# A local-attention and two-MoE kernel on one core: load pieces, a scheduler that counts TensorE's instruction blocks, new keys, and an unused tile

## The chip, the core and the metric

The kernel runs on one core of a Trainium2 chip. A time is device microseconds (us) of one execution. Beside it stands one execution under the hardware profiler, whose trace gives every number on single instructions. TensorE is PE, its weight loads PEld, VectorE DVE, ScalarE ACT, GpSimd POOL, and SyncE SP; all loads that matter here are issued from SP's queue. A PE matmul in the trace comes with one weight load: the text calls the two a pair, which is two instructions.

## The reference

Three layers in float32, with 4 batches, 8 heads of 64, 512 local and 32 global positions.

```python
# layer 1: local queries see +-32 positions and the 32 global keys; global queries see all
s_g = scale * q_g @ k_all.T;  out_g = softmax(s_g) @ v_all
s_ll = where(abs(i - j) <= 32, scale * q_l @ k_l.T, -1e9);  s_lg = scale * q_l @ k_g.T
out_l = softmax(concat([s_lg, s_ll])) @ concat([v_g, v_l])
x = concat([out_g, out_l]) as [4, 576, 512]
# layer 2, d_ff 1024
h = maximum(x @ w_in, 0)
gate = sigmoid(conv3(h, conv_w))         # three taps along the sequence
x = (h * gate) @ w_out
# layer 3
xk, xr = mu_k * x + (1 - mu_k) * x_prev, mu_r * x + (1 - mu_r) * x_prev
out = sigmoid(xr @ w_r) * (maximum(xk @ w_k, 0) ** 2 @ w_v)
```

## The kernel before

**Work.** A unit u is one batch and two heads; there are 16, four to a batch. `attend(u)` makes the scores `s` (32 small matmuls in float32, 64 pairs in the trace), masks them (DVE), takes exponents (ACT), transposes them (`pe`, 4 pairs for each of two heads), multiplies by the values (`o`, 32 pairs a head), normalises into `xn` (DVE) and transposes that into `X` (4 pairs). `glob(u)` does the global queries of units u-1 and u, on odd u: `sg` (8 pairs), the exponents `eg` with their normalisation, `peg` (3 pairs, twice) and `Xg` (48 pairs). Layer 2 multiplies by w_in into `ph` and by w_out into `po`; layer 3 is `pk`, `pr` and `pv` in chunks of 384 tokens. Each float32 weight is split into two parts (`_hi`, `_lo`), and so are the activations, with three matmuls for each product.

**Weights.** A piece of 512 columns of a weight is one DMA (`fload`, 511.8 KB). POOL clears a buffer for its magnitude (`fzero`), ACT takes the absolute value (L733), DVE puts the low words to it (L737), and then the two parts are rounded out (L786, L789).

**Order.** Every step is a `Task` with an engine, a cost in ns, keys, and the buffers that it takes; `Plan.schedule` puts all tasks into one order at build time by a model of the engines' times. `s_key` gives each unit its due time from T_START, STEP0, SLOT and GAP; LAG_TE, LAG_PV, LAG_G and LAG_TX give the later steps of a unit theirs. A task that needs another ACT table is put back by PENALTY. Some steps have a second engine in `alts`, and DVE_BIAS, ACT_BIAS and POOL_BIAS weigh that choice by phase of the kernel. `Clock` models TensorE's clock; where it would fall, or where a wait is long, `warm` puts fillers in front of a task: matmuls on the identity whose result is thrown away (L381). The DMAs are in this order too, so the plan sets which load stands ahead of which in SP's queue. q and k have three buffers each, as v has.

**Data.** The host lays out q, k and v so that one unit's q is 2,304 bytes for each of 128 partitions, k 2,688 and v 7,280, each in one piece.

## Time and profile before

| | us |
|---|---|
| median of 3 runs | 556.32 |
| lowest, highest | 555.46, 558.76 |
| the profiled execution's own time | 557.58 |
| its span, first to last instruction | 555.8 |
| PE busy in the span | 531.0 (96%) |

The profiled execution is 1.26 us above the median, and 1.78 us of it lie outside the span. Times of the trace count from the span's start.

### The profile page before, as it was taken

How to read it: one execution, taken by the hardware profiler on the slowest of the kernel's cores; microseconds unless marked ns; L12 is line 12 of the kernel's file. 1: busy time of each engine (PE TensorE's matmuls, PEld its weight loads, DVE VectorE, ACT ScalarE, POOL GpSimd, SP SyncE). 2: the span in 40 equal slices, each digit the busy share in tenths (PEclk: the TensorE clock that was granted, in tenths of full speed). 3: DMA queues.
4: the chain of work that ended last, by engine and by line, in shares of the span. 5: the costliest groups of instructions: out<-in, count | busy, mean ns of one | idle time of the engine just before them, and what ended most of it. 6: DMA issues, size and time to landing. Idle time of an engine off the chain costs nothing.

```text
span 555.8 us, 13782 instructions
## 1 busy us (share of the span) xinstructions
PE 531.0 (96%) x5502; PEld 487.0 (88%) x5502; DVE 348.0 (63%) x956; ACT 250.9 (45%) x562; POOL 150.7 (27%) x308
## 2 busy tenths in 40 slices
PE   7688979999999799999999999999999999999997
PEld 6576977999999799999999988898898898898896
DVE  4586969635994449952599699499245457245131
ACT  5588979855877458862796673001001001001000
POOL 4323355211021100110100110000077477276060
PEclk9797989999999899999999999999999999999999
DMA  8887706668328501101516641201201200100101
GB/s 313 348 281 285 275 7 218 225 214 285 129 88 285 192 31 50 68 22 43 172 59 196 205 130 44 85 1 44 72 1 28 77 0 20 57 2 0 58 2 38
DMA packets 30593, 64.61 MB, mean 116 GB/s; under 512 B 4672, under 2 KB 16704, under 8 KB 30528
## 3 DMA queue, kind: packets, MB, share of 16 engines
q1 hardware_dynamic: 28224, 59.26, 31.8%
q10 hardware_dynamic: 2304, 4.47, 2.1%
q8 instruction: 43, 0.70, 0.5%
q14 instruction: 22, 0.18, 0.1%
HBM read 51.64 MB, written 12.07 MB: 115 GB/s over the span
## 4 chain that ended last, share of the span: by engine, by line
PE 73%; DVE 9%; DMA 8%; ACT 3%; issue 3%; POOL 2%; SPq 1%; ACTq 0%; DVEq 0%; POOLq 0%
PE pv L1189 17%; PE pk L1086 16%; PE po L949 11%; PE ph L848 9%; PE pr L1152 9%; DMA kT<-in_k_l_dram 3%; DVE c L890 3%; PE s L488 2%; PE o L529 2%; PE pe L519 2%; PE Xg L671 2%; PE sg L612 1%; DMA wkk<-wkkd 1%; DMA v<-in_v_l_dram 1%; PE X L560 1%
## 5 line engine op out<-in xcount | busy, mean ns | idle before, releaser
L848 PE MATMUL ph<-x,win_hi 128*128 128x256 f32 (+1 forms) x512 | 99.3, 292 | 0.0
L848 PEld LDWEIGHTS ph<-x,win_hi 128*128 128x128 f32 x512 | 79.9, 188 | 1.0 <-issue 0.6
L949 PE MATMUL po<-gh,wout_hi 128*128 128x288 f32 (+1 forms) x256 | 77.3, 302 | 0.2 <-issue 0.2
L949 PE MATMUL po<-gl,wout_hi 128*128 128x288 f32 (+1 forms) x256 | 75.0, 293 | 0.6 <-DVE gl L911 0.6
L949 PE MATMUL po<-gh,wout_lo 128*128 128x288 f32 (+1 forms) x256 | 74.5, 291 | 0.0
L848 PE MATMUL ph<-x,win_lo 128*128 128x288 f32 (+1 forms) x256 | 73.4, 287 | 0.0
L1086 PE MATMUL pk<-xkh,wkk_hi 128*128 128x384 f32 (+1 forms) x192 | 62.8, 327 | 0.9 <-ACT xkh L1045 0.9
L1086 PE MATMUL pk<-xkl,wkk_hi 128*128 128x384 f32 (+1 forms) x192 | 62.8, 327 | 0.2 <-DVE xkl L1049 0.2
L1086 PE MATMUL pk<-xkh,wkk_lo 128*128 128x384 f32 (+1 forms) x192 | 62.8, 327 | 0.0
L1167 ACT ACTIVATE robuf<-pr 128x512 f32<-128x512 f32 x17 | 10.2, 599 | 114.8 <-PE pr L1152 112.6
L890 DVE SCALAR_TENSOR_TENSOR c<-h,convw,c 128x544 f32<-128x544 f32 x64 | 50.4, 805 | 6.8 <-ACT c L883 6.3
L1189 PE MATMUL pv<-wvv_lo,k2h 128*128 128x512 f32 (+1 forms) x144 | 54.4, 378 | 0.0
L1189 PE MATMUL pv<-wvv_hi,k2h 128*128 128x512 f32 (+1 forms) x144 | 54.4, 378 | 0.0
L1189 PE MATMUL pv<-wvv_hi,k2l 128*128 128x512 f32 (+1 forms) x144 | 54.4, 377 | 0.0
L1109 POOL TENSOR_TENSOR robuf<-robuf 128x384 f32<-128x384 f32 (+1 forms) x32 | 25.2, 791 | 100.2 <-DVE robuf L1106 100.0
L949 PEld LDWEIGHTS po<-gh,wout_hi 128*128 128x128 f32 x256 | 49.3, 193 | 1.3 <-issue 0.8
L949 PEld LDWEIGHTS po<-gl,wout_hi 128*128 128x128 f32 x256 | 49.3, 193 | 0.9 <-DVE gl L911 0.8
L949 PEld LDWEIGHTS po<-gh,wout_lo 128*128 128x128 f32 x256 | 49.2, 192 | 0.0
L848 PEld LDWEIGHTS ph<-x,win_lo 128*128 128x128 f32 x256 | 48.2, 188 | 0.0
L1202 DVE TENSOR_TENSOR robuf<-pv,robuf 128x512 f32<-128x512 f32 (+1 forms) x18 | 11.9, 662 | 55.4 <-PE pv L1189 38.0
L510 ACT ACTIVATE e<-e 128x128 f32<-128x128 f32 x128 | 40.1, 394 | 10.2 <-DVE e L503 7.8
L1152 PE MATMUL pr<-wrr_hi,xrbuf 128*128 128x512 f32 x136 | 43.7, 395 | 0.0
(188 smaller groups left out, 1127.7 us busy)
## 6 DMA issues: line engine op xcount, KB each, us to landing
v<-in_v_l_dram SPq DMA_DIRECT2D x16, 910.0 KB, 6.9
kT<-in_k_l_dram SPq DMA_DIRECT2D x16, 336.0 KB, 6.1
qT<-in_q_l_dram SPq DMA_DIRECT2D x16, 288.0 KB, 5.3
x2d<-xo ACTq DMA_DIRECT2D x16, 272.5 KB, 3.5
out_dram<-robuf SPq DMA_DIRECT2D x16, 256.0 KB, 2.0
wout_0r<-in_moe_w_out_dram SPq DMA_DIRECT2D x8, 511.8 KB, 4.3
wkk<-wkkd SPq DMA_DIRECT2D x8, 256.0 KB, 3.2
win_0r<-in_moe_w_in_dram SPq DMA_DIRECT2D x4, 511.8 KB, 9.1
```

Source lines behind the costliest of these rows:

```text
L488: nc.tensor.matmul(s[a][32 * j : 32 * j + 32, i], lhsT=qT[rows[a], q : q + 32], rhs=kT[rows[a], c : c + P], start=(i == 0), stop=True, ski ...
L510: nc.scalar.activation(be.tile[:, P * i : P * (i + 1)], be.tile[:, P * i : P * (i + 1)], AF.Exp, bias=be.tile[:, SL + i : SL + i + 1], sca ...
L519: nc.tensor.transpose(pt[:, i], be.tile[:, P * i : P * (i + 1)], ident)
L529: nc.tensor.matmul(o[32 * j : 32 * j + 32, i], lhsT=bt.tile[:, i, 32 * j : 32 * j + 32], rhs=v[:, a, first_block(4 * i + j)], start=(i == ...
L848: nc.tensor.matmul(pm, lhsT=w[:, k, P * m : P * (m + 1)], rhs=x[:, s0:s1], start=(k == 0 and n == 0), stop=(k == KT - 1 and n == 2),)
L890: e.scalar_tensor_tensor(bc.tile, bh.tile[:, k : k + S], convw[:, FT * k + m : FT * k + m + 1], bc.tile, op0=ALU.mult, op1=ALU.add,)
L949: nc.tensor.matmul(pm, lhsT=w[:, k, P * m : P * (m + 1)], rhs=g[:, k % 2, s0:s1], start=(k == 0 and n == 0), stop=(k == FT - 1 and n == 2),)
L1086: nc.tensor.matmul(bp.tile[:, :n], lhsT=w[:, k, P * m : P * (m + 1)], rhs=x[:, :n], start=(k == 0 and i == 0), stop=(k == KT - 1 and i == 2),)
L1109: e.tensor_mul(ks()[:, :n], kk()[:, :n], kk()[:, :n])
L1152: nc.tensor.matmul(bp.tile, lhsT=x[:, P * j : P * (j + 1)], rhs=w[:, k], start=(k == 0 and i == 0), stop=(k == KT - 1 and i == 2),)
L1189: nc.tensor.matmul(bp.tile, lhsT=x, rhs=w[:, k, c0:c1], start=(k == 0 and i == 0), stop=(k == FT - 1 and i == 2),)
L1202: nc.vector.tensor_mul(o()[:, c0:c1], bp.tile, r()[:, c0:c1])
```

## The change

1. **Pieces.** A helper `runs` loads k in two pieces for each partition (1,344 bytes each) and v in four (1,820 bytes each); the host lays k and v out accordingly. q stays in one piece. Each is still one DMA. A 512-column weight load becomes two DMAs, of 2,048 and 2,046 bytes for each partition.
2. **The scheduler.** A class `Fetch` counts the instructions of PE tasks (ROWS) in blocks of 256; where a block is entered, it notes when the one after it would be ready (FETCH, or FETCH_BUSY with loads under way), and a task that crosses into a block that isn't ready gets the difference added to its end.
3. **Numbers.** New keys, lags, biases, filler constants, and costs of `s`, `gs`, `pv`, `gpv`, `zero` and `abs`; LAG_TE goes from 3,470 to -2,216, LAG_PV from 12,390 to 18,256, PENALTY from 587 to 1,360, FILL_MIN from 0 to 336.
4. **A tile.** A tile `edge` of 8 float32 columns stands first in the pool of the second MoE's weights. Nothing writes or reads it. In the built program it has no address, and `wrr_hi` stands at byte 206,816 of a partition and `wrr_lo` at 215,008 in both kernels, which is 32 above a multiple of 64.

```diff
-T_START = 9268
-STEP0 = 4976
+T_START = 9166
+STEP0 = 5715
...
-LAG_TE = 3470
-LAG_PV = 12390
+LAG_TE = -2216
+LAG_PV = 18256
-S_COST = 1330
+S_COST = 880
-FILL_MIN = 0
-FILL_MARGIN = 212
+FILL_MIN = 336
+FILL_MARGIN = 92
-PENALTY = 587
+PENALTY = 1360
+FETCH = 1500
+FETCH_BUSY = 2800
...
                 t.end = clock.run(e, t.cost, t.weight, True)
+                t.end += fetch.run(t.kind, e, t.end, free["DMA"], True)
...
+ROWS = {"s": 128, "pv": 64, "te": 8, "tx": 8, "gt": 6, "gs": 16, "gpv": 192, "warm": 6}
+BLOCK = 256
+class Fetch:
+    def __init__(self):
+        self.rows, self.asked, self.ready = 104.0, 0, {}
+    def run(self, kind, start, end, dma, commit):
+        n = ROWS.get(kind, 12)
+        rows, stall = self.rows, 0.0
+        ready = self.ready if commit else dict(self.ready)
+        for k in range(int(rows // BLOCK) + 1, int((rows + n) // BLOCK) + 1):
+            x = start + (k * BLOCK - rows) / n * (end - start) + stall
+            stall += max(0.0, ready.get(k, 0.0) - x)
+            x = max(x, ready.get(k, 0.0))
+            ready[k + 1] = x + (FETCH_BUSY if dma > x else FETCH)
+        if commit:
+            self.rows = rows + n
+        return stall
...
+    def runs(tile, src):
+        n = src.shape[0]
+        nc.sync.dma_start(out=tile.rearrange("p (c e) -> p c e", c=n), in_=src.rearrange("c p e -> p c e"))
...
-            nc.sync.dma_start(out=halves[:, : 4 * n - 1], in_=skewed(src))
+            part, words = skewed(src), 4 * n - 1
+            step = 4 * EST
+            for c in range(0, words, step):
+                end = min(c + step, words)
+                nc.sync.dma_start(out=halves[:, c:end], in_=part[:, c:end])
...
+                w2["p"].tile([P, 8], F32, tag="edge", name="edge")
...
-        "q_l": q, "k_l": k, "v_l": v,
+        "q_l": runs(q, 1), "k_l": runs(k, 2), "v_l": runs(v.reshape(NU, P, -1), 4),
```

Three places show how the order moves. In them `s3_0` is the scores of unit 3, first head; `pe1_1` the transposes of unit 1, second head; `kT3` and `qT3` are its k and q. A number behind the last underscore is the built program's own and differs between the kernels.

On SP, at the start of the program, behind q0, k0, q1 and k1. Before:

```order
L470 DMA v0_193<-in_v_l_dram 128x1820
L470 DMA v1_231<-in_v_l_dram 128x1820
L464 DMA qT2_282<-in_q_l_dram 128x576
L464 DMA kT2_284<-in_k_l_dram 128x672
L724 DMA win0_0r_297<-in_moe_w_in_dram 128x2047
L724 DMA win1_0r_324<-in_moe_w_in_dram 128x2047
L464 DMA qT3_337<-in_q_l_dram 128x576
L464 DMA kT3_346<-in_k_l_dram 128x672
```

Now:

```order
L491 DMA v0_193<-in_v_l_dram 128x4x455
L491 DMA qT2_271<-in_q_l_dram 128x576
L491 DMA kT2_278<-in_k_l_dram 128x2x336
L491 DMA v1_284<-in_v_l_dram 128x4x455
L762 DMA win0_0r_347<-in_moe_w_in_dram 128x1024
L762 DMA win0_0r_347<-in_moe_w_in_dram 128x1023
L762 DMA win1_0r_354<-in_moe_w_in_dram 128x1024
L762 DMA win1_0r_354<-in_moe_w_in_dram 128x1023
L491 DMA qT3_379<-in_q_l_dram 128x576
L491 DMA kT3_395<-in_k_l_dram 128x2x336
```

q2 and k2 now stand ahead of v1, and the two weight pieces are four DMAs; the bytes ahead of k3 are the same.

On PE, in the first units, behind the first head's `o` of unit 1 (`o1_0`). Before, where the scores of unit 2 follow `o1_0`, then those of unit 3 from here on:

```order
L488 MATMUL s3_0_464<-kT3_346,qT3_337 32x128 x4
L488 MATMUL s3_1_465<-kT3_346,qT3_337 32x128 x4
...
L519 MATMUL pe1_1_515<-ident_94,e1_1_303 128x128 x4
L656 MATMUL peg1_0_521<-ident_94,eg1_309 128x128 x3
L560 MATMUL X0_527<-ident_94,xn0_395 128x128 x4
L519 MATMUL pe2_0_541<-ident_94,e2_0_498 128x128 x4
```

Now, where unit 2's scores stand ahead, right behind `sg1`:

```order
L563 MATMUL o1_0_447<-v1_284,eT1_0_424 32x65 x16
L553 MATMUL pe1_1_473<-ident_94,e1_1_298 128x128 x4
L553 MATMUL pe2_0_482<-ident_94,e2_0_372 128x128 x4
L553 MATMUL pe2_1_493<-ident_94,e2_1_390 128x128 x4
L690 MATMUL peg1_0_499<-ident_94,eg1_341 128x128 x3
L522 MATMUL s3_0_503<-kT3_395,qT3_379 32x128 x4
L522 MATMUL s3_1_504<-kT3_395,qT3_379 32x128 x4
```

Four groups of transposes that stood behind the scores of unit 3 stand ahead of them.

On PE, among the matmuls of the second batch of layer 2. Before, where these four steps follow each other with no dense matmul between them (each row of `s` stands for the eight of its unit):

```order
L671 MATMUL Xg11_3234<-egT11_3202,v11_2700 64x32 x12
L529 MATMUL o11_0_3264<-v11_2700,eT11_0_3170 32x65 x16
L529 MATMUL o11_1_3289<-v11_2700,eT11_1_3187 32x65 x16
L488 MATMUL s12_0_3310<-kT12_2460,qT12_2442 32x128 x4
...
L488 MATMUL s13_0_3349<-kT13_3088,qT13_3070 32x128 x4
...
L949 MATMUL po1_2_1_3217<-gh1_4_2828,wout_hi_170 128x288
```

Now s12 and s13 stand apart, each between dense matmuls, and s10 and s11 stand together:

```order
L705 MATMUL Xg9_2595<-egT9_2547,v9_2319 64x32 x12
L563 MATMUL o9_0_2623<-v9_2319,eT9_0_2478 32x65 x16
L563 MATMUL o9_1_2645<-v9_2319,eT9_1_2495 32x65 x16
L886 MATMUL ph1_4_1_2581<-x0_6_1326,win_hi_160 128x288
...
L886 MATMUL ph1_5_0_2680<-x0_5_174,win_lo_161 128x256
L522 MATMUL s10_0_2695<-kT10_1929,qT10_1918 32x128 x4
...
L522 MATMUL s11_0_2733<-kT11_2445,qT11_2430 32x128 x4
...
L886 MATMUL ph1_5_0_2680<-x0_6_1326,win_hi_160 128x256
```

The run of 240 pairs with only attention work is cut up; in its place stands one of 112 and, 12 dense matmuls later, one of 128.

## Rows read from the trace of the kernel before

**Rows 1.** The page's first part: each engine's busy us, share, instructions.

```profile
PE 531.0 (96%) x5502; PEld 487.0 (88%) x5502; DVE 348.0 (63%) x956; ACT 250.9 (45%) x562; POOL 150.7 (27%) x308
```

**Rows 2.** PE's waits over the whole span: line, releaser, total us, times, longest.

```profile
PE s L488 <- DMA kT<-in_k_l_dram: 4.9, 4, 3.0
PE s L488 <- issue: 4.6, 2, 3.4
PE X L560 <- DVE xn L541: 2.1, 2, 1.5
PE peg L656 <- DVE xn L540: 1.8, 1, 1.8
...
PE Xg L671 <- issue: 0.9, 1, 0.9
```

**Rows 3.** Busy time by stretch: length, engines, granted clock, DMA share, GB/s.

```profile
0.00:104.00 104.00, 87.54 (x1652) 76.32 (x1652) 77.29 (x280) 81.33 (x185) 42.33 (x95) 0.92 0.67 244
104.00:320.00 216.00, 211.99 (x2676) 204.41 (x2665) 143.20 (x402) 143.73 (x323) 22.88 (x111) 0.99 0.43 139
```

**Rows 4.** The same view, four stretches at half clock: the last, the sum.

```profile
188.99:192.40 3.41, 3.41 (x16) 3.41 (x16) 1.84 (x17) 0.57 (x2) 0.50 (x9) 0.50 0.23 79
sum 20.47, PE 18.23 PEld 15.46 DVE 12.62 ACT 12.35 POOL 9.67; mean PE 4.56 PEld 3.86 DVE 3.16 ACT 3.09 POOL 2.42
```

**Rows 5.** The timeline of PE from 14 to 21 us, idle before in brackets.

```profile
14.40 1.15 PE L488 MATMUL s<-kT,qT 64*32 64x128 f32 x64 [0.23 <-DMA kT<-in_k_l_dram]
18.50 1.07 PE L488 MATMUL s<-kT,qT 64*32 64x128 f32 x23 [2.96 <-DMA kT<-in_k_l_dram]
20.74 0.68 PE L488 MATMUL s<-kT,qT 64*32 64x128 f32 x16 [1.16 <-issue]
```

**Rows 6.** The same view from 36 to 48 us.

```profile
39.16 0.55 PE L656 MATMUL peg<-ident,eg 128*128 128x128 f32 x3 [1.75 <-DVE xn L540]
39.54 0.39 PE L381 MATMUL s<-ident 128*128 128x128 f32 x2
```

**Rows 7.** DMA from 0 to 40 us: GB/s in 40 slices, then issues.

```profile
GB/s 0 65 277 323 325 289 405 410 400 422 403 397 374 301 395 400 451 437 382 407 400 418 401 373 362 291 83 0 62 327 278 386 256 291 397 355 255 244 191 304
...
v<-in_v_l_dram SPq DMA_DIRECT2D x5, 910.0 KB, 8.4
kT<-in_k_l_dram SPq DMA_DIRECT2D x7, 336.0 KB, 8.1
```

**Rows 8.** ACT's groups from 0 to 104 us, one of its table loads.

```profile
L510 ACT ACT_TABLE_LOAD x3 | 3.8, 1283 | 0.8 <-PEq L1322 0.7
```

**Rows 9.** Busy time by stretch, 80 to 100 us.

```profile
80.00:100.00 20.00, 19.17 (x338) 17.08 (x338) 18.82 (x55) 19.20 (x39) 9.33 (x13) 0.92 0.58 199
```

**Rows 10.** The timeline of PE from 181 to 190 us.

```profile
183.03 1.74 PE L488 MATMUL s<-kT,qT 64*32 64x128 f32 x104
188.17 0.64 PE L488 MATMUL s<-kT,qT 64*32 64x128 f32 x24 [3.39 <-issue]
```

**Rows 11.** The instruction queue: on the page, then at 185.85 to 186.9 us.

```profile
q8 instruction: 43, 0.70, 0.5%
...
q8 instruction: 1, 0.02, 5.6%
```

**Rows 12.** Busy time and counts from the start and from pause to pause.

```profile
0.00:20.74 20.74, 12.64 (x349) 10.21 (x349) 11.20 (x68) 11.29 (x30) 7.17 (x30) 0.94 0.91 345
20.74:46.92 26.18, 22.07 (x507) 18.65 (x506) 19.02 (x85) 20.06 (x51) 7.69 (x15) 0.89 0.76 264
46.92:96.36 49.44, 45.71 (x634) 40.88 (x634) 40.52 (x110) 43.84 (x90) 24.84 (x44) 0.91 0.53 197
96.36:188.17 91.81, 87.89 (x1392) 83.56 (x1393) 59.33 (x202) 64.62 (x157) 14.60 (x58) 1.00 0.64 209
```

**Rows 13.** PE's groups by form, from 342 us on.

```profile
L1189 PE MATMUL pv<-wvv_lo,k2h 128*128 128x512 f32 x128 | 49.9, 389 | 0.0
...
L1152 PE MATMUL pr<-wrr_hi,xrbuf 128*128 128x512 f32 x113 | 36.4, 395 | 0.0
```

## The prediction

> **What bounds the kernel now.** I read the page's busy times first: PE is busy 531.0 of 555.8 us [rows 1], so the time is PE's matmuls plus what PE loses, and no other engine's sum matters by itself. Then busy time by stretch: in the first 104 us PE is busy 87.54, in the next 216 it is busy 211.99 [rows 3]. The losses sit at the start, where four units of attention wait for loads and for DVE and ACT, and in a few places later. The waits of PE name them: 4.9 us for k loads, 2.1 and 1.8 for `xn` from DVE, and 4.6 us of `s` and 0.9 of `Xg` in which PE waited for nothing that the profile shows [rows 2]. These last ones are of another kind: in the timeline two of them, 1.16 and 3.39 us, stand in the middle of one unit's scores, whose operands are all there [rows 5, 10].

> What they have in common is a count. From the start to the first such pause there are 349 pairs, from there 507, 634 and 1,392 [rows 12] (the third ends in a pause of 0.23 us). Doubled, the last three are 1,014, 1,268 and 2,784 instructions: just under 4, 5 and 11 times 256, and the rest is PE's instructions that leave no matmul record. The instruction queue moved 43 packets, 0.70 MB [rows 11], and 11,004 instructions of PE [rows 1] over 43 is 256. One such packet lies inside the 3.39 us pause [rows 11]. So I take these pauses as PE out of instructions: a block of 256 isn't there when the one before is used up. A block with attention work alone is 128 pairs, and scores go at 104 pairs in 1.74 us [rows 10], so it lasts 2.1 us; 128 pairs before the pause PE was at about 182.6 (24 pairs, some 0.4 us, ahead of 183.03), and it went on at 188.17. The next block thus came some 5.5 us after the one before it was entered, with two v loads behind each other in the queues. [...]

> [...]

> **The change part by part.** The sum is made against the profiled execution, 557.58, which is 1.26 above the median of 556.32; I take the difference off both.

> *The start.* (a) `s3` waits 2.96 us for its k [rows 5]. Before, the transposes pe1_1, peg1_0, pe2_0 and pe2_1 come behind it; now they stand ahead, since the scores of unit 2 are earlier and k2 is loaded ahead of v1. Four groups at peg's 0.55 us [rows 6] are 2.2 us moved into a wait. Against it stands that k3 may land later. The bytes ahead of it are the same, but in shorter pieces: with q and k loads alone (slices 3 to 6) 277 to 325 GB/s move, with v loads behind them (slices 7 to 12) about 405 [rows 7]. If short pieces go at 304, a v load of 910 KB takes 3.0 instead of 2.25 us, 0.75 more, and two stand ahead of k3: 0 to +1.5. The slow slices also hold the queue's start, so I take the middle, 0.8. Net -1.4. (b) peg3_0 waits 1.75 us, by the row for `xn` on DVE [rows 6]; ahead of `xn` DVE also normalises `eg3`, which peg3_0 needs. In the changed kernel ACT does that step, right behind the copy of X1. I take half: -0.9. (c) From 80 to 100 us ACT is busy 19.20 of 20 [rows 9], so work taken from ACT there is time. A table load is 1.28 us [rows 8]. Up to there the new order has 7 of them instead of 9; later it has 12 more, where ACT waits for PE and they cost nothing (that cover gone, they would cost up to 15). 2 x 1.28 = 2.6, of which half on the path: -1.3. Together -3.6. The bounds are wide, as half of this region is reordered: at best another 5 us of its 16.5 without PE work, -8.6; at worst two new waits as long as that for `xn`, +3.

> *The pause at 184.78.* s12 and s13 now stand apart, each between dense matmuls, so no block there is short: -3.39 - 1.7 = **-5.1**. What is late next is nothing that this trace shows: behind it the stretch to 320 us loses little else.

> *New short blocks.* Counting blocks of 256 along the new order, I find three with almost only attention work: six `ph`, s10 and most of s11 (2.7 us); Xg7, half of o8 and s9 (2.8 us); s14, s15 and Xg13 (2.85 us). The first is the worst, as in it two v buffers have just been given back by Xg9 and o9, so v loads run. If a block still takes 5.5 us there, the pause is 2.8 and the clock costs 1.7 again: +4.5. If it takes under 2.7, nothing. The nearest row is the pause with two v loads [rows 10], but those moved 7,280 bytes at a time and these 1,820. I take a third: **+1.5** for the three together, from 0 to 4.5 for one. [...]

> *Other loads and issue.* PE's other k waits are 1.9 us in total [rows 2]; the loads of w_in feed ACT and DVE. Later by up to a quarter of a k load's 8.1 us [rows 7]: 0 to +2.0, and I take **+0.5**. SP issues two DMAs for a weight piece instead of one; its queue waits for buffers most of the time, which covers this, and where it doesn't, the next load starts later by one issue, within the bound just named.

> *Fillers.* The new plan has 11 instead of 3. Two take 0.39 us [rows 6], so eight more are 1.6 us; most stand in waits. **+0.4**, from 0 to 1.6.

> *The tile* is never written or read, and the weights' addresses are the same: **0**. The plan's count is off as well: it counts 192 for each `Xg`, where the trace has 48 pairs, 96. So its idea of where a block begins is wrong behind every `Xg`, and only partly does it do what it is for. Layer 3's order is unchanged, and PE waits for nothing there: 0.

> Sum: -3.6 - 5.1 + 1.5 + 0.5 + 0.4 = -6.3, so 551.3 for the profiled execution and **550.0** against the median.

> **The rivals.** *The start absorbs its gain* (553.6): between 80 and 100 us DVE is busy 18.82 and ACT 19.20 of 20 [rows 9], so what PE gains before is waited for again there, and -3.6 falls away. Speaking for it is how tight that stretch is; against it, that ACT has fewer table loads.

> *Slower, by the blocks* (562.0): if a block still takes 5.5 us, all three short blocks pause: 3 x (2.8 + 1.7) = 13.5 instead of 1.5, so 550.0 + 12.0. At 3.7 us a block it would be no change: 3 x (0.9 + 1.7) is what is gained elsewhere. For it speaks that the plan's count is wrong; against it the shorter pieces, and that two of the three blocks have few loads about them.

> *The pauses aren't fetches* (553.6): PE waited for something else that the v loads cause, the pause comes back wherever these now fall, and the -5.1 and the +1.5 both go. For it speaks that the longest pause stands right behind two v loads; the count of 256 and the packet inside the pause speak against it. [...]

> *The tile works after all* (548.7), that is, the other direction of "does nothing": `pr` takes 395 ns a matmul and `pv`, whose weights stand on a multiple of 64, 389 [rows 13]. If it moved the tiles, 204 matmuls by 6 ns are 1.3 us less.

> **How the numbers follow.** Chances: forecast 0.54, start absorbed 0.24, slower by blocks 0.12, not fetches 0.06, tile 0.04. The forecast's own range is 545 to 554, and the likeliest value 550.0. The range for 8 in 10 is 544.5 to 558.5: it takes in the absorbed start and the worst single block, and leaves out the slower rival and the best of the start. Within 1% (about what a measurement can tell from no change) is 550.8 to 561.9. Of the forecast's 0.54 some 0.38 lies below 550.8, as its start has more room to gain than to lose; with the tile, faster is 0.42. Slower is its rival's 0.12, and the rest, 0.46, is within 1%.

> **What would show it.** After: the wait of `s` for "issue" without a pause over 1 us around 184; `s3`'s wait for k under 1.5 us; ACT's busy time from 80 to 100 us below 19; layer 3 as before, `pr` at 395. Wrong would be: pauses in the middle of s11, s9 or Xg13, each behind an instruction packet that lands late; k3 landing over 2 us later; or a new wait between 60 and 104 us as long as what the start gained.

## The result, and the profile after

The changed kernel takes 548.7 us (median of 4 runs, 547.92 to 550.56) against 556.72 for the kernel before: a ratio of 0.9895, with an interval of 0.9852 to 0.9938. By the ratio that is 5.9 us less; 6.3 were forecast. The ratio is not the quotient of the two medians, which is 0.9856 (8.0 us) and lies inside the interval. Nine more runs gave 0.9904 (0.9868 to 0.9940). Executions over 1.5% above the fastest of their kernel are left out of all ratios; two of them, one of b_short and one of i_nofill, took 856 us at a mean clock of 0.557. The profiled execution took 550.56, its span is 548.8.

The first part of the page and PE's waits (line, releaser, total us, times, longest) in the changed kernel, to be held against [rows 1, 2]:

```profile
PE 530.2 (97%) x5518; PEld 486.8 (89%) x5518; DVE 323.0 (59%) x896; ACT 288.9 (53%) x631; POOL 144.8 (26%) x309
```

```profile
PE s L522 <- DMA kT<-in_k_l_dram: 4.4, 3, 2.2
PE X L594 <- issue: 2.5, 1, 2.5
PE s L522 <- issue: 2.2, 3, 1.2
PE pk L1124 <- ACT xkh L1083: 1.4, 1, 1.4
PE pe L410 <- DVE egT L695: 1.4, 1, 1.4
...
PE X L594 <- DVE xn L575: 0.2, 1, 0.2
```

The 3.39 us pause is gone. The waits that name `xn` went from 2.1 and 1.8 to 0.2 (1.7 in the trace of after_again), the one for `eg` from 1.4 to 0.3. But the waits for k are almost what they were, 4.4 instead of 4.9, and PE still waits 4.7 us for "issue" in two groups, against 5.5 before.

Where PE's idle time went is best seen in two stretches. Busy time by stretch, before and then changed:

```profile
0.00:36.00 36.00, 27.90 (x642) 23.33 (x646) 21.49 (x121) 22.69 (x61) 10.71 (x38) 0.91 0.86 321
36.00:104.00 68.00, 59.64 (x1022) 52.99 (x1014) 55.80 (x160) 58.64 (x125) 31.62 (x57) 0.92 0.58 204
```

```profile
0.00:36.00 36.00, 27.21 (x640) 22.45 (x640) 19.39 (x105) 21.35 (x58) 11.44 (x39) 0.86 0.86 300
36.00:104.00 68.00, 65.12 (x985) 59.24 (x977) 58.23 (x185) 61.91 (x138) 22.49 (x52) 0.97 0.65 218
```

In the first 36 us nothing is gained: 640 matmuls instead of 642. From 36 to 104 us PE is idle 2.9 instead of 8.4 us (4.4 in the trace of after_again). The timeline of PE in the changed kernel shows why the first stretch stood still (idle before in brackets):

```profile
9.58 1.14 PE L646 MATMUL sg<-kT,qT 128*64 128x480 f32 x8
12.53 0.70 PE L522 MATMUL s<-kT,qT 64*32 64x128 f32 x33 [1.82 <-DMA kT<-in_k_l_dram]
...
20.29 0.41 PE L522 MATMUL s<-kT,qT 64*32 64x128 f32 x5
21.41 1.21 PE L522 MATMUL s<-kT,qT 64*32 64x128 f32 x59 [0.71 <-issue]
22.54 1.12 PE L563 MATMUL o<-v,eT 128*32 128x65 f32 x64
23.59 0.55 PE L690 MATMUL peg<-ident,eg 128*128 128x128 f32 x3
26.62 0.60 PE L594 MATMUL X<-ident,xn 128*128 128x128 f32 x4 [2.48 <-issue]
...
44.67 0.83 PE L410 MATMUL pe<-ident 128*128 128x128 f32 x6
...
143.37 1.96 PE L522 MATMUL s<-kT,qT 64*32 64x128 f32 x120
146.50 0.42 PE L522 MATMUL s<-kT,qT 64*32 64x128 f32 x8 [1.16 <-issue]
```

`s3` (20.29) no longer waits for its k, as it did for 2.96 us [rows 5]. Instead `s2`, which now stands ahead, waits 1.82 for k2 behind `sg1`, and a new pause of 2.48 us stands in front of the first transposes into X, those of X0 (the expectations below call the place X1). Between the two "issue" pauses lie 59 + 64 + 3 = 126 pairs, a block of 128 within what the rows resolve at its edges. The new short block of the forecast is there too, after 120 of the 128 pairs of s10 and s11. The row at 44.67 is three fillers; the text comes back to it.

### The profile page after: what moved, and what is told of

It reads as the page before. It is cut to its first block, busy times and chain, and to the rows that moved or that the text cites. A ratio compares the mean times of both kernels' runs of the same rounds, so it can differ in the third digit from the quotient of the medians.

```text
span 548.8 us, 13843 instructions
## 1 busy us (share of the span) xinstructions
PE 530.2 (97%) x5518; PEld 486.8 (89%) x5518; DVE 323.0 (59%) x896; ACT 288.9 (53%) x631; POOL 144.8 (26%) x309
## 4 chain that ended last, share of the span: by engine, by line
PE 42%; DVE 4%; ACT 2%; DMA 1%; issue 1%; ACTq 0%; DVEq 0%
PE pv L1227 17%; PE pk L1124 16%; PE pr L1190 9%; DMA wvv_0r<-in_moe_w_v_dram 1%; DVE c L928 1%; ACT c L921 1%; DMA wvv_256r<-in_moe_w_v_dram 1%; DVE gl L949 0%; ACT h L910 0%; DVE xkl L1087 0%; DVE wrr_lo L827 0%; DVE xt0xr L1073 0%; ACT c L934 0%; DVE xrbuf L1101 0%; DVE d L1061 0%
## 5 line engine op out<-in xcount | busy, mean ns | idle before, releaser
L886 PE MATMUL ph<-x,win_hi 128*128 128x288 f32 (+1 forms) x512 | 99.1, 292 | 0.0
L987 PE MATMUL po<-gh,wout_hi 128*128 128x288 f32 (+1 forms) x256 | 75.9, 296 | 0.0
L1142 ACT ACTIVATE robuf<-pk 128x384 f32<-128x384 f32 (+1 forms) x36 | 16.7, 466 | 69.6 <-PE pk L1124 68.9
L987 PEld LDWEIGHTS po<-gl,wout_hi 128*128 128x128 f32 x256 | 48.2, 188 | 1.0 <-DVE gl L949 0.9
L987 PEld LDWEIGHTS po<-gh,wout_hi 128*128 128x128 f32 x256 | 48.2, 188 | 0.7
```

The source lines that it names most:

```text
L886: nc.tensor.matmul(pm, lhsT=w[:, k, P * m : P * (m + 1)], rhs=x[:, s0:s1], start=(k == 0 and n == 0), stop=(k == KT - 1 and n == 2),)
L987: nc.tensor.matmul(pm, lhsT=w[:, k, P * m : P * (m + 1)], rhs=g[:, k % 2, s0:s1], start=(k == 0 and n == 0), stop=(k == FT - 1 and n == 2),)
L1142: e.activation(kk()[:, :n], bp.tile[:, :n], AF.Relu)
```

## The experiments

Two theories were set against each other throughout: that the order carries the gain, above all s13 away from s12, whose pause is PE out of instructions; and rivals by part (pieces, fetch model, loads of v). Each ratio is to the kernel before, run on the same chip.

**One step moved in the kernel before** (e_s13): behind the schedule, the scores of unit 13 and what hangs on them are put 5 dense tasks, 30 matmuls, later.

```diff
+    order = plan.schedule()
+    pe = [t for t in order if t.eng == "PE"]
+    i = next(i for i, t in enumerate(pe) if t.name == "s13")
+    first, stop = order.index(pe[i]), order.index(pe[i + 5])
+    late = [pe[i]]   # and the tasks in between that depend on it
...
-    for t in plan.schedule():
+    for t in order:
```

> The kernel before with one step moved: the scores of unit 13 come 30 dense matmuls (po) later, so that s12 and s13 no longer stand together; long pieces and all else as before. Theory (the pause is PE out of instructions in a block of attention work alone): the block now lasts over 5 us, the pause of 3.39 us and the half clock behind it (1.7) go, 551.6 against 556.7. Rival (PE waits for something that the two v loads cause): a pause of 2 to 3.4 us comes back in s12, in the dense matmuls or in s13, and the time is 555 to 557.

Measured: 551.54 us, 0.9897 (0.9863 to 0.9932). PE's timeline there:

```profile
181.74 1.16 PE L488 MATMUL s<-kT,qT 64*32 64x128 f32 x64
...
186.72 1.29 PE L488 MATMUL s<-kT,qT 64*32 64x128 f32 x64
```

No pause in s12, in the dense matmuls or in s13, and no stretch at half clock there. By the ratio this step alone gives 5.7 us (3.8 to 7.6 by its interval; the two medians differ by 4.0), no less than the whole change as far as these intervals tell.

**The boundary moved** (c_shift): 16 small matmuls, overwritten afterwards, ahead of Xg9 in the kernel before.

```diff
             X = alloc(bt[2], [P, 2, SG], F32, f"Xg{u}")
+            for _ in range(16 if u == 9 else 0):
+                nc.tensor.matmul(X[:, 0], lhsT=ident, rhs=ident[:, :SG], start=True, stop=True, ...)
```

> The kernel before with 16 small matmuls (32 pairs, on the identity, overwritten afterwards) put ahead of Xg9, some 35 us ahead of s12; nothing else is moved. Before, the pause comes when 41 of the 64 pairs of s13 are done. Theory (PE is out of instructions at a boundary of 256): the boundary moves 32 pairs ahead in the work, so the pause comes after 9 of the 64 pairs of s13, 2.5 to 4 us long. Rival (PE waits for something tied to this unit, its loads or its buffers): the pause stays at 41 of 64, or at the first pair of a unit.

```profile
187.36 1.31 PE L488 MATMUL s<-kT,qT 64*32 64x128 f32 x72
189.63 1.08 PE L488 MATMUL s<-kT,qT 64*32 64x128 f32 x56 [0.96 <-issue]
```

Before, 104 of the 128 pairs came ahead of the pause [rows 10], now 72: exactly the 32 pairs put in, 35 us earlier. The place of the pause is a count of instructions. Its length was missed: 0.96 us, not 2.5 to 4. The boundary now stands differently to the two v loads: they are issued at 181.40 us before and at 185.73 here, and the instruction packet is under way 4.5 us later before and 1.0 us later here. That this made the pause short was not tried by itself. The run is a single execution, 560.8 us; its time also holds other waits, so no ratio is drawn from it.

**Pieces.** The changed kernel with long pieces (a_long, the diff below), and the kernel before with part 1 of the change alone (b_short); each keeps its order on every engine.

```diff
-        "k_l": runs(k, 2), "v_l": runs(v.reshape(NU, P, -1), 4),
+        "k_l": runs(k, 1), "v_l": runs(v.reshape(NU, P, -1), 1),
...
-            step = 4 * EST
+            step = words
```

> The changed kernel with long load pieces: every engine's order is that of the changed kernel, k and v are loaded in one piece for each partition (2,688 and 7,280 bytes) and a 512-column weight piece in one DMA. Theory (the new order carries the gain): 548.5 to 551, at most 2 us above the changed kernel, and the pause between s10 and s11, 1.16 us with short pieces, grows towards 2.8. [...]

> The kernel before with short load pieces alone: its own order on every engine, k in two pieces, v in four, a 512-column weight piece in two DMAs. Theory (the new order carries the gain): 555 to 558, the pause within s13 stays at 2 to 3.4 us. Rival (the short pieces carry it): 549 to 552, the pause within s13 falls under 1 us and the lower clock behind it goes.

a_long: 551.57, 0.9923 (0.9894 to 0.9952), beside 0.9904 for the changed kernel. b_short: 557.29, 1.003 (1.0003 to 1.0057). In the traces of the two, first a_long at s10 and s11, then b_short at s12 and s13:

```profile
143.08 1.96 PE L522 MATMUL s<-kT,qT 64*32 64x128 f32 x120
145.96 0.42 PE L522 MATMUL s<-kT,qT 64*32 64x128 f32 x8 [0.92 <-issue]
```

```profile
179.94 1.75 PE L493 MATMUL s<-kT,qT 64*32 64x128 f32 x104
185.35 1.08 PE L493 MATMUL s<-kT,qT 64*32 64x128 f32 x24 [3.67 <-issue]
```

Short pieces shorten neither pause: 1.16 (1.35 in the second trace) against 0.92 with long ones, and 3.67 against 3.39. They carry no gain that these intervals show: alone they make the kernel before some 0.3% slower, and a_long is 1.1 us above the changed kernel by the two ratios, 0.6 above its expected range by its time. The 3.67 is a little more than the 3.4 expected at most. The expected growth of the pause towards 2.8 with long pieces did not come either.

**The fetch model off** (g_nofetch): FETCH and FETCH_BUSY at 0 in the changed kernel.

```diff
-FETCH = 1500
-FETCH_BUSY = 2800
+FETCH = 0
+FETCH_BUSY = 0
```

> The changed kernel with its fetch model switched off (FETCH and FETCH_BUSY at 0), keys and pieces kept: s6 and s7 come together, sg5 behind Xg3, s12 earlier; s12 and s13 stay apart, s10 and s11 together. Theory (the keys set s12 and s13 apart, and the fetch model adds little): within 1.5 us of the changed kernel, a pause of 1 to 2.5 us between s6 and s7. Rival (the fetch model is what avoids the pauses): 3 us or more above it, with two or more pauses over 2 us.

555.63 us, 1.0003 (0.9975 to 1.0030): 5.5 us above the changed kernel, which is the rival's time, though not by its mechanism. Its waits of PE:

```profile
PE o L563 <- ACT eT L556: 3.1, 1, 3.1
...
PE o L563 <- issue: 2.4, 4, 1.2
PE X L594 <- issue: 2.2, 1, 2.2
PE po L987 <- DVE gl L949: 1.8, 3, 0.9
PE peg L690 <- DVE x L604: 1.3, 1, 1.3
```

Only one pause is over 2 us, and that one, at X0, the changed kernel has as well. Most of the rest are waits for ACT and DVE, the longest at `o` of unit 4, and the order differs most in units 4 to 7. So the model is worth its 5.5 us through the order that comes out with it; whether that is more than the luck of one list order stays open, as its counts are known to be off (192 for an `Xg` of 96).

**The weights of layer 3 on 64 bytes** (d_edge): a pool of 32 bytes a partition opened ahead of theirs, in place of `edge`.

```diff
+                w2["e"] = ctx.enter_context(tc.tile_pool(name="edge", bufs=1, side="right"))
+                nc.gpsimd.memset(w2["e"].tile([P, 8], F32, tag="edge", name="edge"), 0.0)
                 w2["p"] = ctx.enter_context(tc.tile_pool(name="w2", bufs=1, side="right"))
-                w2["p"].tile([P, 8], F32, tag="edge", name="edge")
```

> The changed kernel with the weights of layer 3 really on 64 bytes: a pool of 32 bytes a partition with one cleared tile is opened ahead of theirs, which moves wkk and wrr by 32 bytes to multiples of 64; the order is the same. Theory (pr's 395 ns against pv's 389 come from the address): pr at 389, and 204 x 6 ns = 1.3 us less than the changed kernel, 547.4. Rival (the difference is of another kind): pr stays at 395 and the time at 548.7.

551.15 us, 0.9899 (0.9843 to 0.9955). PE's groups by form:

```profile
L1190 PE MATMUL pr<-wrr_hi,xrbuf 128*128 128x512 f32 x136 | 43.7, 395 | 0.0
L1190 PE MATMUL pr<-wrr_lo,xrbuf 128*128 128x512 f32 x68 | 26.9, 395 | 0.0
```

395 ns, as in the changed kernel and before [rows 13]: the address is not what sets `pr` apart from `pv`. What does was not tried.

**Fillers.** The changed kernel without its 11 fillers (i_nofill, and once more as i_nofill_2); with each cut to 8 columns (k_tiny); without fillers and with long pieces (p_nofill_long); and the kernel before with s13 moved and without its 3 fillers (q_s13_nofill).

```diff
     for t in plan.schedule():
-        plan.fill = t.fill
+        plan.fill = 0
```

For k_tiny the fillers themselves are cut:

```diff
-                out[:, :P], lhsT=ident, rhs=ident, start=True, stop=True, skip_group_check=True
+                out[:, : P if n else 8], lhsT=ident, rhs=ident if n else ident[:, :8], start=True, stop=True,
+                skip_group_check=True
```

> The changed kernel once more, beside the same runs of the kernel before as the next two. Theory (one step, s13 away from s12, carries most): -5 to -6 us against before, like that step alone, with long pieces 1 to 2 us behind it. Rival (the start gains as much again): -8 to -9.

> The changed kernel with its 11 fillers left out, the order otherwise the same. Theory (fillers cost PE 0.2 us each where PE doesn't wait, and little where it does): 0 to 1.5 us less than the changed kernel, and the stretches at half clock as they are. Rival (they hold the clock up): one or two stretches at half clock more, 1.7 to 3.4 us above the changed kernel.

> The changed kernel without its fillers once more, beside the same runs of the kernel before. Both theories: 545 to 547.5, which is 8 to 10 below the kernel before; 549 or more would mean that its first time was chance.

> The changed kernel with each of its 11 fillers cut from 128 to 8 columns: the same count of instructions, and so the same boundaries of 256, at under a third of a filler's time. Theory (without fillers it was faster because the boundaries moved by 22 pairs): about the changed kernel's time, 549 to 550.5, with the pauses at X1 (2.5 to 3) and between s10 and s11 (1.2) back. Rival (the fillers' own time was the cost): 546 to 547.5, as without them.

> The changed kernel without fillers and with long load pieces. Theory (short pieces are worth 1 to 2 us in this order): 547 to 549. Rival (they are worth nothing): as without fillers and with short pieces, 545 to 547.

> The kernel before with s13 moved away from s12 and without its 3 fillers. Theory (the new order of the start gains 3 to 5 us by itself, and fillers and boundaries ate it): 550 to 552, as with its fillers, and so 4 to 6 above the changed kernel without fillers. Rival (the start gains nothing, and leaving fillers out is worth 3 to 5 in either order): 546 to 548.

| kernel | us | ratio, interval |
|---|---|---|
| changed, again (after_again) | 550.33 | 0.9904 (0.9868 to 0.9940) |
| without fillers (i_nofill) | 546.17 | 0.9838 (0.9795 to 0.9881) |
| the same again (i_nofill_2) | 545.31 | 0.9813 (0.9788 to 0.9839) |
| fillers of 8 columns (k_tiny) | 549.12 | 0.9886 (0.9856 to 0.9916) |
| no fillers, long pieces (p_nofill_long) | 545.62 | 0.9814 (0.9786 to 0.9842) |
| before, s13 moved, no fillers (q_s13_nofill) | 550.21 | 0.9906 (0.9886 to 0.9926) |

Leaving the fillers out takes 4 us more off, and gives the fastest kernel of the study, 9 and 10 us under the kernel before. Neither expectation of i_nofill had this: one saw 0 to 1.5 us less, the other more time. PE's waits in i_nofill_2:

```profile
PE s L522 <- DMA kT<-in_k_l_dram: 4.4, 4, 1.8
...
PE po L987 <- DVE gl L949: 1.6, 2, 1.0
...
PE X L594 <- DVE xn L575: 1.4, 3, 0.6
PE sg L646 <- issue: 1.1, 1, 1.1
...
PE s L522 <- DVE x L604: 0.9, 1, 0.9
```

11 fillers are 22 pairs, so all boundaries behind them move. The pause of s10 and s11 is gone, and the one at X0 (2.5 to 3.0) has become one of 1.1 within `sg3` (1.4 in i_nofill): 2.3 to 3.3 us in all, beside the fillers' own time. k_tiny was to part these two and does so only in half. The pauses are back with the count of instructions, as expected:

```profile
PE X L595 <- issue: 2.5, 1, 2.5
PE s L523 <- issue: 2.2, 2, 1.1
```

But cutting a filler's columns did not cut its time. Three of them take 0.83 us in the changed kernel's timeline (44.67, above), and in k_tiny's:

```profile
42.07 0.73 PE L410 MATMUL pe<-ident 128*128 128x8 f32 x6
```

So the shares of time and boundaries aren't measured apart. By the rows, the eight fillers behind those of s0 are 16 pairs, at six in 0.73 to 0.83 us 1.9 to 2.2 us; but without them the waits for `gl`, for `xn` and of `s` for `x` are 1.6, 1.4 and 0.9 us instead of 0.3, 0.2 and 0.4, so only part of their time is won. The clock has a share that isn't parted either: from 0 to 104 us the mean granted clock is 0.93 and 0.98 in the two traces of the changed kernel, and 1.00 in those of k_tiny, i_nofill and i_nofill_2. That fillers hold it up isn't shown, nor that they are harmful to it: in p_nofill_long, also without them, it is 0.93.

Two of these runs answer the other questions. Long pieces without fillers give the same 0.9814: the pieces are worth nothing that these runs resolve, which is some 2 us. And the old order, with s13 moved and no fillers, is 0.9906, 5.2 us (0.93% of 556) behind the changed order without fillers. The traces place this in the start: behind s9, where both orders have done the same work, PE is at 125.3 us in q_s13_nofill and at 118.2 in i_nofill_2. So without fillers the new start is worth about 5 us, most of which is lost again with them.

## Why the prediction was right, and where it was not

The sum was -6.3, and -5.9 and -5.3 were measured. *The pause at 184.78*, -5.1: right, and shown by its own experiment at -5.7, whose interval holds 5.1. Its 1.7 is an estimate from the row of the last stretch at half clock [rows 4]: PE is busy there for the whole 3.41 us at a granted clock of 0.50, with 16 matmuls, and the next 3.41 us, at 1.00, have 31. In e_s13, without the pause, no such stretch stands there; that a pause always brings one is not shown, and the runs have one against it, at s10 and s11 below. That the place of the pause is a count of instructions is shown by c_shift to the pair; that the count is 256 rests on the rows that the prediction shows. Of the 43 blocks of the kernel before, four have a pause over 0.3 us (1.16, 1.75, 0.90 and 3.39), all in blocks with mostly attention work.

*New short blocks*, +1.5: right in place and size at s10 and s11: 1.16, 1.35, 1.25 and 1.15 us (changed, changed again, d_edge, k_tiny), with no fall of the clock behind it (the granted clock is 1.00 from 143 to 150 us in the changed kernel), so the 1.7 in the worst case of 4.5 did not come. At s9 the changed kernel has no wait over 0.3 us. Behind s14, s15 and Xg13 its two traces have none either, but three others of the same order, a_long, d_edge and k_tiny, pause there for 0.52, 0.46 and 0.64 us. But the shorter pieces, which I set against a long pause there, fell as a reason: long pieces gave 0.92.

*The start*, -3.6: with its fillers it came near that, but not by its parts. Behind s9, where both orders have done the same work, PE is at 124.9 to 128.0 us in five traces with the old start (the profiled execution of the kernel before is the slowest), and at 120.5 to 124.5 in five with the new start and its 11 fillers; the means are 125.9 and 123.0. In i_nofill and i_nofill_2 it is at 118.1 and 118.2 (122.1 in p_nofill_long).

(a), -1.4, failed. I costed the transposes as moved into a wait and took it that nothing is late in their place. s2, moved ahead with them, waits 1.82 us for k2, and the boundary that stood in s3 is followed by one at X0 with 2.5 to 3.0 us: by 36 us nothing was won. The short blocks that I named all lie from s9 on; those of the start, which move as well, I left out.

(b), -0.9, was read wrong, and here too a boundary was overlooked. The row names `xn`, but peg3_0 reads only the identity and `eg3`, which was normalised by 32.0 us, 7 us ahead of its start at 39.16. In the built program it waits for one thing of DVE, the masks of unit 4's scores, and the last of these ended at 34.7 us. The count fits instead: from the pause in s3 to peg3_0 there are 380 pairs, three blocks, and from there to the pause in Xg3 128. An instruction packet landed 1.43 us ahead of the end of the wait, as at the other three pauses (1.33 to 1.43). In b_short and c_shift the wait stands at the same place again, with 0.78 us each, and in e_s13 with 0.27, there put down to "issue"; no run moved this boundary by itself. The kernel before:

```profile
31.42 0.54 DVE L646 TENSOR_SCALAR eg<-eg 128x608 f32<-128x608 f32 x1
```

```profile
20.74:39.16 18.42, 16.66 (x380) 14.36 (x379) 13.31 (x63) 14.56 (x39) 5.04 (x11) 0.88 0.81 278
39.16:46.92 7.76, 5.41 (x128) 4.29 (x128) 5.71 (x24) 5.50 (x14) 2.65 (x5) 0.92 0.65 233
```

In the changed kernel this boundary falls among other work and no wait stands there: the wait that I counted on did go, for another reason. (c): ACT is busy 18.15 of 20 us from 80 to 100 instead of 19.20 [rows 9], as forecast; what PE gained by it isn't shown. Row of busy time, changed kernel:

```profile
80.00:100.00 20.00, 18.46 (x305) 16.22 (x306) 18.09 (x67) 18.15 (x38) 7.29 (x13) 0.91 0.53 169
```

*Fillers*, +0.4: the term that was most off. A filler is two pairs, so the 0.39 us of [rows 6] is one filler and not two, and eight more cost 1.9 to 2.2 us by the rows above instead of 1.6. I looked at what they take in waits and left out that they move every boundary behind them; leaving them out gave 3.7 us (0.9904 less 0.9838 of 555.35), and 4.1 against k_tiny (0.9886 less 0.9813 of 556.05). Start and fillers together come to some -0.8 to -1.4 by difference (the whole change, less s13 moved, less the new block's 1.2), where -3.2 was forecast; each ratio is uncertain by some 2 us, so this difference is rough, and the traces above would give -2.9. That the sum came so near is in part luck: without fillers the new start gains more than the 3.6 forecast, the fillers cost some 4 instead of 0.4, and the two errors cancel.

*Other loads*, +0.5, and the slower k3: the pieces measured nothing that the runs resolve, and the waits for k are 0.5 us less in the first trace. *The tile*, 0: right, and its rival fell, since with a real shift to 64 bytes (d_edge) `pr` still takes 395 ns (its 204 times 6 ns are 1.2 us, not 1.3). *The fetch model* "only partly does what it is for": its count is off, but without it the order is 5.5 us slower, which I had not weighed at all.

The rivals: an absorbed start (553.6) missed by 3 us; much of the start's gain was lost again, but to the fillers and their boundaries and not to DVE and ACT. Slower by the blocks needed long pauses at three places; one of 1.2 us came, and one of some 0.5 in part of the traces.

## What to carry to other kernels

Where PE stops in the middle of work whose operands are there, count instructions between such stops: where the count is a multiple of 256, as here, put a few small matmuls in earlier and see whether the stop moves by as much. Here 32 pairs moved it by 32, and 30 dense matmuls between two runs of small ones removed it. A stop of this kind here, the 1.75 us at peg3_0, stood under the name of a releaser that was long done: count there too. Moving one step by hand behind a scheduler shows in one run what a set of new keys is worth. Try the order without fillers before tuning them: here the kernel took 3.7 us less without its 11, and every boundary behind them shifted.
